# Key sums on TensorE, nine gradient steps ahead of the attention loop, and other queues for stores and transposes

## The chip, the cores and the metric

The kernel runs on one core of one Trainium2 chip. The core has five engines with instruction queues of their own: TensorE (PE in the profile; its weight loads are PEld), VectorE (DVE), ScalarE (ACT), GpSimd (POOL) and SyncE (SP), which here only issues DMAs. Sixteen DMA engines move the data. The metric is the device time of one execution in microseconds, as a median of several runs; less is better.

## The reference

The reference is one transformer block with linear attention and a gated feed-forward network (FFN), and its full backward pass. Tokens S = 2048, width D = 640, H = 32 heads of 20, FFN width F = 1728, all in bfloat16. The forward part, cut to what matters here:

```python
qkv = split_heads(layernorm(x) @ wqkv)              # q, k, v
phi = lambda t: jnp.where(t > 0, t + 1, jnp.exp(t)) + 1e-6
pq, pk = phi(q), phi(k)
kv  = jnp.einsum("bhsd,bhse->bhde", pk, v)
z   = jnp.einsum("bhsd->bhd", pk)                    # sum over all tokens
num = jnp.einsum("bhqd,bhde->bhqe", pq, kv)
den = jnp.einsum("bhqd,bhd->bhq", pq, z)[..., None] + 1e-6
h   = x + merge_heads(num / den) @ wo
xh  = layernorm(h)
h2  = h + (silu(xh @ w_gate) * (xh @ w_up)) @ w_down
```

`jax.vjp` then takes a given `grad_out` back to x and the five weight matrices. The seven outputs are h2 and these six gradients.

## The kernel before

The 2048 tokens are 16 tiles of 128. Matrices stay in SBUF as bfloat16 with 128 partitions; products are made in four PSUM tiles (`mm`, tag "mm"), which all stages share, each two banks wide. A PSUM tile is free again when ScalarE or VectorE has read it.

The stages in order of time are these.

1. Layer norm of x, q and k for each token tile, and phi (the loop that ends at line 379). `pk` holds phi(k), `pqa` holds phi(q). The function `phi(which, t, n)` works on n token tiles on VectorE, and after each fourth tile issues stores of the result from SyncE.
2. The sum z over all tokens, on VectorE (lines 465 to 472): FP32 additions over pairs of token tiles, a halving, and a split into a bfloat16 value `zs[0]` and a rest `zs[1]`. `z_bcast` multiplies both by a matrix of ones on TensorE, which puts z on all partitions (`zb`). Beside it TensorE makes Y = xn^T pk (`ps_y`, five row blocks), from it `KVT` (`ps_kvt`, lines 502 to 514, masked to heads by VectorE) and from that the combined matrix `W2` (`ps_w2t`, then a DMA transpose).
3. The normalisation of phi(q) by the denominator, four token tiles at a time: `norm_den` and `norm_mul`, on VectorE. `tr_pqs` then transposes the normalised tiles into `pqsT` with DMAs issued by SyncE.
4. The attention loop (lines 539 to 581). For each token tile t: ten matmuls `ps_a`; VectorE adds x (`xr`, loaded by SyncE) and so makes h in place, then layer-norm statistics; GpSimd makes the reciprocal deviation; two tiles later VectorE makes `hn` and SyncE transposes it into `hnT`. h itself goes to DRAM (`scr_h1`), issued by GpSimd. An `xr` buffer is free for the next load once `hn` is made and the store of h has landed; there are six buffers of that tag.
5. The FFN, in four column groups g of 448, 448, 448 and 384 columns (lines 603 to 704), starting with `pg`, then the backward pass.

Between the matmuls of stages 2 to 4 stand 24 *dm steps* (`dm_steps`, lines 393 to 407): each multiplies two token tiles of the transposed `grad_out` by a column group of `w_down`^T (`ps_dm`, 20 matmuls), and ScalarE copies the result out of PSUM. Groups 0 and 1 have 448 columns and stay in SBUF; the last eight steps have 384 columns and go to DRAM by a store that ScalarE issues (`scr_dm`, line 406). `dm(n)` puts n steps at a place in TensorE's order: twelve stand ahead of the attention loop, one between the halves of its first tile, and eleven in the loop, where t = 3, 7, 11 and 15 have none.

The order of the work on an engine is written out by hand in blocks (`manual_schedule`) for the engines that the block names: there the instructions run in the order of the program. On the other engines, and between two such blocks, a scheduler places them. `load_wgu(0)`, the first FFN weights, is written behind the loop; its two buffers are those of `wdT` and `wdT3`, the weights of the dm steps, so it needs step 16 to have run.

Of the kernel before, what the change touches and what calls it, by code (L numbers as in the profile page):

```python
# [8 lines left out]
FP32 = mybir.dt.float32  # L9
BF16 = mybir.dt.bfloat16  # L10
ALU = mybir.AluOpType
# [9 lines left out]
def kernel(  # L21
# [208 lines left out]
    with tc.manual_schedule(engines={EngineType.Pool}):  # L230
        ident = const.tile([P, P], BF16, name="ident")
        make_identity(nc, ident[:])
        nhalf = const.tile([P, 4], FP32, name="nhalf")
        nc.vector.memset(nhalf[:], -0.5)
        ones = const.tile([P, P], BF16, name="ones")
        nc.vector.memset(ones[:], 1.0)
        E = const.tile([P, D], BF16, name="E")
    zpad = const.tile([P, 4, 64], BF16, name="zpad")
    nc.vector.memset(zpad[:], 0.0)
    mask = const.tile([P, 160], BF16, name="mask")  # L240
# [67 lines left out]
    def phi(which, t, n=2):  # L308
        e = (pk, pqa)[which][:, t:t + n, :]
        nc.vector.tensor_scalar(out=e, in0=e, scalar1=1.0, scalar2=1e-6, op0=ALU.min, op1=ALU.add)  # L310
        last = nc.vector.tensor_tensor(out=e, in0=e, in1=rr[:, 2 * which + t // 2 % 2, t % 2:t % 2 + n, :], op=ALU.add)
# [7 lines left out]
        return last.ins  # L319

    PIECES = ((0, 3), (3, DT))

    with tc.manual_schedule(engines={EngineType.PE, EngineType.DVE, EngineType.Activation, EngineType.Pool}):
# [33 lines left out]
        for t in range(2, ST):  # L357
            if t == 2:
                ln1_stats(4)
            if t > 3 and t + 3 < ST:  # L360
                ln1_stats(t + 3)
            kq_mm(t, 0, (lambda: copy1(t + 1)) if t + 1 < ST else None)
            if t == 2:
                ln1_stats(5)
            if t == 3:
                ln1_stats(6)
            if t == ST - 1:
                phi(0, t - 1, 1)
            kq_mm(t, 1)
            if t == 3:  # L370
                phi(1, 0)
            elif t == ST - 1:
                last_phi = phi(0, t, 1)
            elif t > 3:
                phi(t % 2, t - 2 - t % 2)
            if t + 2 < ST:
                ln1_xn(t + 2)
            if ST - NC - 1 <= t < ST - 1:
                ln1_xn(t - ST + NC + 1)

    dm_t = {0: strips.tile([P, ST, GM], BF16, name="dm0", tag="S")}

# [26 lines left out]
    def dm(n):  # L411
        for _ in range(n):
            next(dms, None)

    def masks():
        nc.gpsimd.memset(mask[:], 1.0)
        for c0, n, p0 in ((0, 6, 0), (120, 2, 88)):
            m = mask[:, c0:c0 + n * Dh]
            for sign in (1, -1):
                nc.gpsimd.affine_select(  # L420
                    out=m, in_=m, pattern=[[-sign * Dh, n], [0, Dh]], compare_op=ALU.is_ge, fill=0.0,
                    base=-p0 if sign > 0 else p0 + Dh - 1, channel_multiplier=sign)
# [7 lines left out]
    def hb4(ap):  # L430
        return ap.rearrange("p t (h e) -> p t h e", e=Dh)

    def norm_den(t):

        pq = pqa[:, t:t + 4, :]
        tz = tzs[:, t % 8:t % 8 + 4, :]
        nc.vector.tensor_tensor(out=tz, in0=pq, in1=zb[:].unsqueeze(1).to_broadcast([P, 4, D]), op=ALU.mult)
        den = small.tile([P, 4, H], FP32, name="den", tag="den", bufs=2)
        nc.vector.tensor_reduce(out=den[:], in_=hb4(tz), axis=AX.X, op=ALU.add)
        nc.vector.tensor_scalar(out=den[:], in0=den[:], scalar1=1e-6, scalar2=None, op0=ALU.add)  # L440
        nc.vector.reciprocal(out=rall[:, t:t + 4, :], in_=den[:])

    def norm_mul(t):
        pq = pqa[:, t:t + 4, :]
        nc.vector.tensor_tensor(out=hb4(pq), in0=hb4(pq), in1=bc4(rall[:, t:t + 4, :]), op=ALU.mult)

    def tr_pqs(t, n=4):
        for tt in range(t, t + n):
            nc.sync.dma_start_transpose(out=pqsT[:, :, tt * P:(tt + 1) * P], in_=pqa[:, tt, :])

    xrs = {}
# [3 lines left out]
            xrs[t] = wk("xr")  # L455
            nc.sync.dma_start(out=xrs[t][:], in_=x_v[:, t, :])

    with tc.manual_schedule(engines={EngineType.PE, EngineType.DVE, EngineType.SP, EngineType.Pool}):
        yk = strips.tile([P, DT * D + HG * P], BF16, name="yk", tag="S")
        Yt = yk[:, :DT * D].rearrange("p (k n) -> p k n", k=DT)  # L460
        KVT = yk[:, DT * D:].rearrange("p (j c) -> p j c", j=HG)
        z2 = tzs[:, 4:8].rearrange("p t d -> p (t d)").bitcast(FP32)
        zf = z2[:, :D]
        tok2 = pk.rearrange("p (t two) d -> p t (two d)", two=2)
        with tc.issue_after(last_phi):
            nc.vector.tensor_tensor(out=z2, in0=tok2[:, 0], in1=tok2[:, 1], op=ALU.add)
        for t in range(2, ST // 2):
            nc.vector.tensor_tensor(out=z2, in0=z2, in1=tok2[:, t], op=ALU.add)
        nc.vector.tensor_tensor(out=zf, in0=zf, in1=z2[:, D:], op=ALU.add)
        zs = [wk("zs"), wk("zl")]  # L470
        nc.vector.tensor_copy(out=zs[0][:], in_=zf)
        nc.vector.tensor_tensor(out=zs[1][:], in0=zf, in1=zs[0][:], op=ALU.subtract)
        for t in (ST - 4, ST - 2):
            phi(1, t)
        nc.vector.memset(KVT, 0.0)
        masks()

        def z_bcast():
            ps = mm("ps_zb")
            mm_row(ps, lambda k: ones[:], lambda k, n0, n1: zs[k][:, n0:n1], 2)  # L480
            nc.scalar.copy(out=half(zb[:]), in_=row(ps))
# [38 lines left out]
        for i in range(DT):  # L520
# [15 lines left out]
        h1s = {}  # L536
        h1_todo = []
        hnT_todo = []
        for t in range(ST + 2):
            if t < ST:  # L540
                xr = xrs.pop(t)
# [11 lines left out]
                h1_todo.append((t, xr))  # L553
# [12 lines left out]
            u = t - 2  # L566
            if u < 0:
                continue
# [15 lines left out]
    fA.close()  # L584
    fpool = wB.enter_context(tc.tile_pool(name="fpool", bufs=6))

    with tc.manual_schedule(engines={EngineType.SP}):
        dh2 = big.tile([P, ST, D], BF16, name="dh2", tag="B")
# [477 lines left out]
```

## Time and profile before

| what | value |
|---|---|
| median of 3 runs | 822.23 us (821.71 to 822.48) |
| the profiled execution | 821.71 us, its span 820.0 us |
| TensorE busy (PE) | 812.0 us, 99% of the span |
| VectorE busy (DVE) | 453.0 us, 55% |
| ScalarE busy (ACT) | 288.1 us, 35% |
| GpSimd busy (POOL) | 200.4 us, 24% |
| mean granted TensorE clock | 0.998 |
| DMA, mean over the span | 193 GB/s |
| DMA in 55 to 85 us | busy share 0.37, 114 GB/s |
| DMA in 118 to 124 us | busy share 1.00, 291 GB/s |
| DMA in 150.2 to 183 us | busy share 1.07, 204 GB/s |

The span is the time from the first to the last instruction; what the execution takes beyond it is its start and end. The stages have their own limits, so the mean shares say little about one of them. In the views that follow, a line of the order of time gives the start in us, the length in us, the engine, the line of the kernel, the operation, the tile written and the tile read, the shape and the number of instructions; in square brackets stands how long the engine was idle before it and what ended that. A "q" behind an engine's name is its queue, which waits and issues DMAs.

### The profile page before, as it was taken

The numbers are of one execution on the slowest core, as the hardware profiler recorded it, in microseconds if no ns is written. First come the engines' busy times: TensorE is split into PE (matmuls) and PEld (weight loads), VectorE is DVE, ScalarE is ACT, GpSimd is POOL, SyncE is SP. The second block draws the span as 40 slices with busy tenths as digits, with TensorE's granted clock in tenths as the row PEclk, the third lists the DMA queues.
The fourth block names the chain that finished last, engine by engine and source line by source line (L and its number), as shares of the span: only waits on it lengthen the run. The fifth ranks groups of instructions, "written<-read, shape, count | busy, mean of one in ns | idle before, by whom it ended". The sixth has DMA issues, their size and how long they took to land.

```text
span 820.0 us, 13924 instructions
## 1 busy us (share of the span) xinstructions
PE 812.0 (99%) x5508; PEld 522.5 (64%) x5508; DVE 453.0 (55%) x857; ACT 288.1 (35%) x405; POOL 200.4 (24%) x366
## 2 busy tenths in 40 slices
PE   9999998999999999999999999999999999999998
PEld 7776565545555555555566677777777777777676
DVE  7879986891078008810670148787793266631212
ACT  6972531570085025500741122322322133322010
POOL 4410043412422311221124611221120111112330
PEclk9999999999999999999999999999999999999999
DMA  9992789999859976894398757987498999999952
GB/s 302 198 327 72 171 185 264 223 210 210 217 141 210 235 202 135 212 263 94 97 222 192 264 119 207 232 199 191 99 259 164 176 144 187 170 186 267 258 151 79
DMA packets 276785, 158.61 MB, mean 193 GB/s; under 512 B 235052, under 2 KB 262829, under 8 KB 276720
## 3 DMA queue, kind: packets, MB, share of 16 engines
q1 hardware_dynamic: 251696, 82.12, 53.8%
q0 software_dynamic: 18512, 67.07, 26.1%
q10 hardware_dynamic: 6512, 8.54, 3.3%
q8 instruction: 43, 0.70, 0.3%
q14 instruction: 22, 0.18, 0.1%
HBM read 47.68 MB, written 53.66 MB: 124 GB/s over the span
## 4 chain that ended last, share of the span: by engine, by line
PE 94%; DMA 4%; DVE 1%; issue 0%; ACT 0%; SPq 0%; POOL 0%; DVEq 0%; POOLq 0%
PE ps_dw L684 21%; PE ps_dhn L109 14%; PE ps_dxn L936 8%; PE ps_o L998 7%; PE pg L612 6%; PE ps_kq L300 5%; PE ps_dwqk L109 5%; PE pu L617 5%; PE ps_dm L390 5%; PE ps_dk L109 3%; PE ps_gt L743 3%; PE ps_dp L109 3%; PE ps_y L487 3%; PE ps_a L545 2%; PE pdm L390 2%; DMA stg<-dd 2%
## 5 line engine op out<-in xcount | busy, mean ns | idle before, releaser
L109 PE MATMUL ps_dhn<-wgT,cols 128*128 128x320 bf16 x864 | 119.5, 299 | 0.0
L684 PE MATMUL ps_dw<-dd,hn 128*128 128x448 bf16 (+1 forms) x640 | 118.8, 346 | 0.0
L109 PEld LDWEIGHTS <-cols 128*128 128x128 bf16 x864 | 84.5, 98 | 32.9
L684 PEld LDWEIGHTS <-hn 128*128 128x128 bf16 x640 | 62.6, 98 | 54.2
L686 DVE CAST dwev<-ps_dw 128x896 bf16<-128x896 f32 (+3 forms) x12 | 10.9, 907 | 128.3 <-PE ps_dw L684 110.2
L649 POOL DMA_DIRECT2D scr_dT<-stg x64 | 34.6, 541 | 167.4 <-DMA stg<-dd 166.9
L686 ACT CAST dwev<-ps_dw 128x896 bf16<-128x896 f32 (+1 forms) x20 | 17.6, 878 | 160.0 <-PE ps_dw L684 151.2
L147 DVE CUSTOM_DVE_ANT_0 lb_a<-lb_dy,hn 128x640 bf16<-128x640 bf16 x32 | 26.4, 826 | 76.1 <-ACT lb_dy L145 76.1
L617 PE MATMUL pu<-wgu,hnT 128*128 128x448 bf16 (+1 forms) x320 | 63.6, 346 | 0.0
L612 PE MATMUL pg<-wgu,hnT 128*128 128x448 bf16 (+1 forms) x320 | 63.6, 346 | 0.0
L998 PE MATMUL ps_o<-wd,mT 128*128 128x320 bf16 (+3 forms) x462 | 61.1, 295 | 0.0
L684 PE MATMUL ps_dw<-m_s,dh 128*128 128x448 bf16 (+1 forms) x320 | 60.5, 346 | 0.4 <-DMA dh<-in_grad_out_dram 0.4
L936 PEld LDWEIGHTS <-ring 128*128 128x128 bf16 x480 | 47.0, 98 | 18.2
L998 PEld LDWEIGHTS <-mT 128*128 128x128 bf16 (+1 forms) x462 | 41.8, 97 | 17.4 <-issue 2.6
L936 PE MATMUL ps_dxn<-wqkvT,ring 128*128 128x320 bf16 x320 | 51.3, 299 | 0.0
L390 PE MATMUL ps_dm<-wdT,dh2T 128*128 128x448 bf16 (+1 forms) x240 | 47.5, 348 | 3.2 <-DVE xr L549 3.2
L390 PEld LDWEIGHTS <-dh2T 128*128 128x128 bf16 x320 | 31.2, 98 | 28.8 <-issue 4.0
L684 PEld LDWEIGHTS <-dh 128*128 128x128 bf16 x320 | 31.2, 98 | 27.8 <-DMA dh<-in_grad_out_dram 0.9
L617 PEld LDWEIGHTS <-hnT 128*128 128x128 bf16 x320 | 31.3, 98 | 27.1
L612 PEld LDWEIGHTS <-hnT 128*128 128x128 bf16 x320 | 31.3, 98 | 27.0
L300 PE MATMUL ps_kq<-wqk,xnT 128*128 128x320 bf16 x320 | 46.4, 299 | 0.0
L145 ACT ACTIVATE lb_dy<-ps_dhn,rstd 128x640 bf16<-128x640 f32 x16 | 12.7, 793 | 86.7 <-PE ps_dhn L109 86.7
(168 smaller groups left out, 1294.5 us busy)
## 6 DMA issues: line engine op xcount, KB each, us to landing
scr_dT<-stg POOLq DMA_DIRECT2D x48, 224.0 KB, 3.2
cols<-scr_dT POOLq DMA_DIRECT2D x6, 1728.0 KB, 9.1
scr_m<-m_s POOLq DMA_DIRECT2D x12, 448.0 KB, 4.6
cols<-scr_dT ACTq DMA_DIRECT2D x2, 1728.0 KB, 10.4
out_dram<-dwev POOLq DMA_DIRECT2D x30, 112.0 KB, 3.2
scr_dT<-stg POOLq DMA_DIRECT2D x16, 192.0 KB, 2.7
scr_pk<-pk SPq DMA_DIRECT2D x4, 640.0 KB, 7.0
scr_xnT<-xnT SPq DMA_DIRECT2D x4, 640.0 KB, 7.2
```

What stands on the lines that cost most here:

```text
L109: nc.tensor.matmul(ps[:, ci, :320], lhsT=lhs(k), rhs=rhs(k, *NCH[ci]), start=(start and k == 0), stop=(stop and k == n - 1))
L147: nc.vector.tensor_tensor_reduce(out=a[:], in0=dy[:], in1=xhat, scale=1.0, scalar=0.0, op0=ALU.mult, op1=ALU.add, accum_out=sums[:, 1:2])
L300: nc.tensor.matmul(ps[:, ci, :320], lhsT=xnT[:, t, k, :], rhs=wqk[:, k, w0 + n0:w0 + n1], start=(k == 0), stop=(k == DT - 1))
L390: nc.tensor.matmul(ps[:, c, :w], lhsT=dh2T[:, kt, (t + c) * P:(t + c + 1) * P], rhs=wdT[:, kt, o:o + w], start=(kt == 0), stop=(kt == DT - 1))
L487: nc.tensor.matmul(ps[:, ci, :320], lhsT=xn[:, t, i * P:(i + 1) * P], rhs=pk[:, t, n0:n1], start=(t == 0), stop=(t == ST - 1))
L612: nc.tensor.matmul(pg[:, c, :w], lhsT=hnT[:, kt, (t + c) * P:(t + c + 1) * P], rhs=wg[:, kt, 0:w], start=(kt == 0), stop=(kt == DT - 1))
L617: nc.tensor.matmul(pu[:, c, :w], lhsT=hnT[:, kt, (t + c) * P:(t + c + 1) * P], rhs=wg[:, kt, w:2 * w], start=(kt == 0), stop=(kt == DT - 1))
L649: nc.gpsimd.dma_start(out=scr_dT[t + c, :, KO[g]:KO[g] + GK[g], :], in_=stg[:, :GK[g], :])
L684: nc.tensor.matmul(ps[:, c, :w], lhsT=lhs(t), rhs=rhs(t), start=(t == 0), stop=(t == ST - 1))
L686: last = copy(out=ev[:, :len(parts), :w], in_=ps[:, :len(parts), :w])
L936: nc.tensor.matmul(ps[:, ci, :320], lhsT=lhs[:, i, :], rhs=rhs[:, i, n0:n1], start=(k == 0 and i == 0), stop=(k == 2 and i == DT - 1))
L998: nc.tensor.matmul(po(t, ci), lhsT=mTs[t // 4][r, t % 4, j, :], rhs=wd[r, j, n0:n1], start=(t, ci) not in opened, stop=last)
```

## The change

The diff does the following.

- z is summed by TensorE: 32 matmuls with 32 columns of ones as weights, four quarters of the PSUM partitions in turn, between the halves of the first `ps_y` block. All 32 rows of a quarter hold the same sum, so the broadcast uses ones divided by 32 (`ones32`). ScalarE and VectorE make the split into `zs[0]` and `zs[1]` from PSUM. The FP32 additions on VectorE are gone.
- The last two `phi(1, ...)` run in the first stage's loop, ahead of the z work.
- The head masks are built on GpSimd, kept in the program's order, after the broadcast.
- `norm_den` and `norm_mul` become one function, `normalise`. Tiles 0 to 7 are normalised and transposed before the `xr` loads and `ps_kvt`, tiles 8 to 15 after `ps_w2t`; all transposes into `pqsT` are issued ahead of the loop.
- Nine dm steps stand ahead of the loop instead of twelve; in the loop there is one after each tile until the 24 are used up.
- The store of h (`scr_h1`) is issued by ScalarE at step t = u + 2, instead of by GpSimd a tile later than it is made.
- `hnT` is allocated ahead of the loop, and each tile of it is transposed in the step in which its `hn` is made. Before, the first four steps issued none, and later ones up to two.
- GpSimd's order in this part is no longer by hand. The pool `fpool` is opened, and `fA` closed, before the dm steps.

```diff
@@ (constants)
+    ones32 = const.tile([P, P], BF16, name="ones32")
+    nc.vector.memset(ones32[:], 1.0 / H)
@@ (first stage, in the loop over t)
             elif t == ST - 1:
-                last_phi = phi(0, t, 1)
+                phi(0, t, 1)
+                phi(1, t - 3)
+                phi(1, t - 1)
...
+    fA.close()
+    fpool = wB.enter_context(tc.tile_pool(name="fpool", bufs=6))
...
-    def norm_den(t):
+    def normalise(t):
...
-    def norm_mul(t):
-        pq = pqa[:, t:t + 4, :]
         nc.vector.tensor_tensor(out=hb4(pq), in0=hb4(pq), in1=bc4(rall[:, t:t + 4, :]), op=ALU.mult)
...
-    with tc.manual_schedule(engines={EngineType.PE, EngineType.DVE, EngineType.SP, EngineType.Pool}):
+    with tc.manual_schedule(engines={EngineType.PE, EngineType.DVE, EngineType.SP}):
...
-        with tc.issue_after(last_phi):
-            nc.vector.tensor_tensor(out=z2, in0=tok2[:, 0], in1=tok2[:, 1], op=ALU.add)
-        for t in range(2, ST // 2):
-            nc.vector.tensor_tensor(out=z2, in0=z2, in1=tok2[:, t], op=ALU.add)
-        nc.vector.tensor_tensor(out=zf, in0=zf, in1=z2[:, D:], op=ALU.add)
         zs = [wk("zs"), wk("zl")]
-        nc.vector.tensor_copy(out=zs[0][:], in_=zf)
-        nc.vector.tensor_tensor(out=zs[1][:], in0=zf, in1=zs[0][:], op=ALU.subtract)
-        for t in (ST - 4, ST - 2):
-            phi(1, t)
-        nc.vector.memset(KVT, 0.0)
-        masks()
...
+        def z_sum():
+            ps = mm("ps_z")
+            for ci, (n0, n1) in enumerate(NCH):
+                for t in range(ST):
+                    q = t % 4 * H
+                    nc.tensor.matmul(ps[q:q + H, ci, :320], lhsT=ones[:, :H], rhs=pk[:, t, n0:n1],
+                                     start=(t < 4), stop=(t >= ST - 4))
+            nc.scalar.copy(out=half(zs[0][:]), in_=row(ps))
+            nc.vector.tensor_tensor(out=half(zs[1][:]), in0=row(ps), in1=half(zs[0][:]), op=ALU.subtract)
+            nc.vector.memset(KVT, 0.0)
...
-                if (i, ci) == (2, 1):
-                    z_bcast()
+                if (i, ci) == (0, 0):
+                    z_sum()
             nc.scalar.copy(out=half(Yt[:, i, :]), in_=row(ps))
+            if i == 0:
+                ps_z = mm("ps_zb")
+                mm_row(ps_z, lambda k: ones32[:], lambda k, n0, n1: zs[k][:, n0:n1], 2)
+                nc.scalar.copy(out=half(zb[:]), in_=row(ps_z))
+                masks()
             if 0 < i < 4:
                 dm(1)
         dm(1)
-        norm_den(0)
-        norm_mul(0)
-        tr_pqs(0)
-        norm_den(4)
+        for t in (0, 4):
+            normalise(t)
+            tr_pqs(t)
         for t in range(6):
             load_xr(t)
...
-        norm_mul(4)
...
-        tr_pqs(4)
         for t in (8, 12):
-            norm_den(t)
-            norm_mul(t)
-            if t < 12:
-                tr_pqs(t)
-        dm(5)
+            normalise(t)
+            tr_pqs(t)
+        dm(2)
 
         hn = big.tile([P, ST, D], BF16, name="hn", tag="B")
+        hnT = big.tile([P, DT, S], BF16, name="hnT", tag="B")
...
-                if t > 0 and t % 4 != 3:
+                if t > 0:
                     dm(1)
-            while h1_todo and h1_todo[0][0] < t:
-                v, h1 = h1_todo.pop(0)
-                nc.gpsimd.dma_start(out=scr_h1_v[:, v, :], in_=h1[:])
             if t > 2:
                 load_xr(t + 3)
-            if t < 4:
-                tr_pqs(12 + t, 1)
-            if t == 3:
-                hnT = big.tile([P, DT, S], BF16, name="hnT", tag="B")
...
             h1, mv = h1s.pop(u)
+            nc.scalar.dma_start(out=scr_h1_v[:, u, :], in_=h1[:])
             nc.vector.tensor_scalar(out=hn[:, u, :], in0=h1[:], scalar1=mv[:, 0, 0:1],
                                     scalar2=rstd2[:, u:u + 1], op0=ALU.subtract, op1=ALU.mult)
-            hnT_todo.append(u)
-            for v in hnT_todo[:0 if t < 4 else 2]:
-                hnT_todo.pop(0)
-                nc.sync.dma_start_transpose(out=hnT[:, :, v * P:(v + 1) * P], in_=hn[:, v, :])
+            nc.sync.dma_start_transpose(out=hnT[:, :, u * P:(u + 1) * P], in_=hn[:, u, :])
```

More of the change, by code (lines that the diff above doesn't have):

```diff
@@ L310, in phi @@
         nc.vector.tensor_scalar(out=e, in0=e, scalar1=1.0, scalar2=1e-6, op0=ALU.min, op1=ALU.add)
-        last = nc.vector.tensor_tensor(out=e, in0=e, in1=rr[:, 2 * which + t // 2 % 2, t % 2:t % 2 + n, :], op=ALU.add)
+        nc.vector.tensor_tensor(out=e, in0=e, in1=rr[:, 2 * which + t // 2 % 2, t % 2:t % 2 + n, :], op=ALU.add)
         if (t + n) % 4 == 0:
@@ L318, in phi @@
                 nc.sync.dma_start(out=scr_xnT[sl].rearrange("t p k c -> p t k c"), in_=xnT[:, sl])
-        return last.ins
     PIECES = ((0, 3), (3, DT))
@@ L415, in masks @@
     def masks():
-        nc.gpsimd.memset(mask[:], 1.0)
+        tc.keep_in_program_order(nc.gpsimd.memset(mask[:], 1.0))
         for c0, n, p0 in ((0, 6, 0), (120, 2, 88)):
@@ L419, in masks @@
             for sign in (1, -1):
-                nc.gpsimd.affine_select(
+                tc.keep_in_program_order(nc.gpsimd.affine_select(
                     out=m, in_=m, pattern=[[-sign * Dh, n], [0, Dh]], compare_op=ALU.is_ge, fill=0.0,
-                    base=-p0 if sign > 0 else p0 + Dh - 1, channel_multiplier=sign)
+                    base=-p0 if sign > 0 else p0 + Dh - 1, channel_multiplier=sign))
     pqsT = big.tile([P, DT, S], BF16, name="pqsT", tag="B")
@@ L441, in norm_den, with tr_pqs @@
         nc.vector.reciprocal(out=rall[:, t:t + 4, :], in_=den[:])
-    def norm_mul(t):
-        pq = pqa[:, t:t + 4, :]
         nc.vector.tensor_tensor(out=hb4(pq), in0=hb4(pq), in1=bc4(rall[:, t:t + 4, :]), op=ALU.mult)
-    def tr_pqs(t, n=4):
-        for tt in range(t, t + n):
+    def tr_pqs(t):
+        for tt in range(t, t + 4):
             nc.sync.dma_start_transpose(out=pqsT[:, :, tt * P:(tt + 1) * P], in_=pqa[:, tt, :])
@@ L461 @@
         KVT = yk[:, DT * D:].rearrange("p (j c) -> p j c", j=HG)
-        z2 = tzs[:, 4:8].rearrange("p t d -> p (t d)").bitcast(FP32)
-        zf = z2[:, :D]
-        tok2 = pk.rearrange("p (t two) d -> p t (two d)", two=2)
-        with tc.issue_after(last_phi):
-            nc.vector.tensor_tensor(out=z2, in0=tok2[:, 0], in1=tok2[:, 1], op=ALU.add)
-        for t in range(2, ST // 2):
-            nc.vector.tensor_tensor(out=z2, in0=z2, in1=tok2[:, t], op=ALU.add)
-        nc.vector.tensor_tensor(out=zf, in0=zf, in1=z2[:, D:], op=ALU.add)
-        zs = [wk("zs"), wk("zl")]
-        nc.vector.tensor_copy(out=zs[0][:], in_=zf)
-        nc.vector.tensor_tensor(out=zs[1][:], in0=zf, in1=zs[0][:], op=ALU.subtract)
-        for t in (ST - 4, ST - 2):
-            phi(1, t)
-        nc.vector.memset(KVT, 0.0)
-        masks()
[L478 to L481, printed above, removed]
+        zs = [wk("zs"), wk("zl")]
+        def z_sum():
[8 more added lines that the diff above has]
+            nc.vector.memset(KVT, 0.0)
         for i in range(DT):
@@ L526 @@
             nc.sync.dma_start_transpose(out=W2[:, :, i * P:(i + 1) * P], in_=W2T[:, i, :])
-        tr_pqs(4)
         for t in (8, 12):
-            norm_den(t)
-            norm_mul(t)
-            if t < 12:
-                tr_pqs(t)
-        dm(5)
+            normalise(t)
+            tr_pqs(t)
+        dm(2)
         hn = big.tile([P, ST, D], BF16, name="hn", tag="B")
+        hnT = big.tile([P, DT, S], BF16, name="hnT", tag="B")
         h1s = {}
-        h1_todo = []
-        hnT_todo = []
         for t in range(ST + 2):
@@ L552 @@
                 ln_rstd(mv, rstd2, t, 1)
-                h1_todo.append((t, xr))
                 h1s[t] = (xr, mv)
-                if t > 0 and t % 4 != 3:
+                if t > 0:
                     dm(1)
-            while h1_todo and h1_todo[0][0] < t:
-                v, h1 = h1_todo.pop(0)
-                nc.gpsimd.dma_start(out=scr_h1_v[:, v, :], in_=h1[:])
             if t > 2:
                 load_xr(t + 3)
-            if t < 4:
-                tr_pqs(12 + t, 1)
-            if t == 3:
-                hnT = big.tile([P, DT, S], BF16, name="hnT", tag="B")
             u = t - 2
@@ L575 @@
             h1, mv = h1s.pop(u)
+            nc.scalar.dma_start(out=scr_h1_v[:, u, :], in_=h1[:])
             nc.vector.tensor_scalar(out=hn[:, u, :], in0=h1[:], scalar1=mv[:, 0, 0:1],
                                     scalar2=rstd2[:, u:u + 1], op0=ALU.subtract, op1=ALU.mult)
-            hnT_todo.append(u)
-            for v in hnT_todo[:0 if t < 4 else 2]:
-                hnT_todo.pop(0)
-                nc.sync.dma_start_transpose(out=hnT[:, :, v * P:(v + 1) * P], in_=hn[:, v, :])
-    fA.close()
-    fpool = wB.enter_context(tc.tile_pool(name="fpool", bufs=6))
+            nc.sync.dma_start_transpose(out=hnT[:, :, u * P:(u + 1) * P], in_=hn[:, u, :])
     with tc.manual_schedule(engines={EngineType.SP}):
```

## The prediction

> **What bounds the kernel now.** I read the waits of TensorE first, then the chain of waits, then stretches of the attention loop, then its instructions in order of time. The waits of TensorE, with total, number and longest in us, are these:
>
> ```profile
> PE ps_dm L390 <- DVE xr L549: 3.2, 1, 3.2
> PE ps_warm L329 <- POOL ident masks.py:199: 1.6, 1, 1.6
> PE ps_dw L684 <- DMA dh<-in_grad_out_dram: 0.4, 1, 0.4
> ```
>
> TensorE is busy for 99% of the span, so every matmul added is paid for in full, and what another engine saves counts only where TensorE waits. The second of these waits is the start of the kernel and the third the first weight gradient; inside the changed part it waits once, for 3.2 us. The chain (start, length) gives the places around it and the price of one kind of matmul that the change adds:
>
> ```profile
> 93.49 9.46 PE ps_dm L390 x50
> 150.26 1.91 PE pg L612 x10
> 618.82 1.20 PE ps_dz L876 x32
> ```
>
> The attention loop begins at 93.49 + 9.46 = 102.95 and the FFN at 150.26, so it takes 47.31. Its matmuls need less. The chain shows a half tile `ps_a` of ten matmuls as 1.36, a `ps_dm` step as 1.89 at 448 columns and about 1.63 at 384. Sixteen tiles (21.76), four steps of 1.89 and eight of 1.63 make 42.36. So 4.95 us are lost. Where they go is seen in the loop (stretch, length, busy us of each engine, granted clock, DMA share, GB/s):
>
> ```profile
> 133.00:136.00 3.00, 3.00 (x23) 2.09 (x22) 0.21 (x1) 0.00 (x0) 1.46 (x3) 1.00 1.11 196
> 136.00:140.00 4.00, 0.83 (x7) 0.43 (x5) 1.37 (x3) 0.80 (x1) 0.00 (x0) 1.00 1.16 285
> 140.00:145.00 5.00, 5.00 (x24) 2.77 (x23) 4.83 (x13) 0.80 (x1) 2.92 (x6) 0.66 0.99 289
> ```
>
> From 133 VectorE and ScalarE nearly stop, the DMA engines are full, TensorE stops at 136.3, and then it works at a granted clock of 0.66. The gap is 3.17, so the slow clock is the other 1.8. The Trainium skill ("TensorE: Matmul & The Clock Gate", Part 1) says that an idle window of about 3.4 us halves the clock until TensorE has been busy again; the trace agrees with the halving, after a gap of 3.17, and by that rule a gap well under a window would cost its own length alone. In order of time:
>
> ```profile
> 127.07 0.61 SPq L185 DMA_DIRECT2D wgu<-in_B_w_gate_dram  x1
> 127.73 0.74 SPq L186 DMA_DIRECT2D wgu<-in_B_w_up_dram  x1
> 130.63 0.86 SPq L456 DMA_DIRECT2D xr<-in_A_x_dram  x1
> 131.27 0.80 ACT L404 CAST dmst<-ps_dm 128x768 bf16<-128x768 f32 x1 [2.82 <-DMA xr<-in_A_x_dram]
> 133.42 2.88 PE L545 MATMUL ps_a<-wvo,pqsT 128*128 128x320 bf16 x20
> 137.72 0.37 ACTq L406 DMA_DIRECT2D scr_dm<-dmst  x1
> 138.59 0.82 DVE L549 TENSOR_TENSOR xr<-ps_a,xr 128x640 bf16<-128x640 f32 x1 [5.38 <-DMA xr<-in_A_x_dram]
> 139.47 2.73 PE L390 MATMUL ps_dm<-wdT,dh2T 128*128 128x384 bf16 x10 [3.17 <-DVE xr L549]
> ```
>
> SyncE issues the first FFN weights at 127.07 and 127.73 (1.1 MB), and the `xr` load for tile 10 behind them at 130.63. The chain has that load as 7.84 long, so it lands at 138.47. VectorE could have added tile 10 about 133.2 and adds it at 138.59; TensorE has meanwhile filled all four PSUM tiles (two attention tiles stand side by side at 133.42, since the step at t = 11 is left out) and takes up step 139.47 when the add ends.
>
> **The change, part by part.** *z on TensorE.* Seven FP32 adds, a half add, a cast and a subtraction leave VectorE: 1.48 + 9.12 + 0.83 + 0.49 + 0.82 = 12.7 us, from 55.74 to 68.63, all beside matmuls, so nothing is saved directly. TensorE gains 32 matmuls of 32 weight columns. The same shape, `ps_dz`, takes 1.20 for 32; as 32 full-width ones (`ps_y`, 4.35 for 32) it would be 4.35. The new ones write the four quarters in turn as `ps_dz` does, so I take **+1.20**, and keep +4.35 as the other end. The Trainium skill ("TensorEngine Tiling", Key Properties) says that a change of tiling mode drains TensorE; a quarter of 4.35 is 1.09, so in this trace such drains have at most 0.11 for `ps_dz`, already inside the row.
>
> The broadcast of z (four matmuls, 0.54, in both) now waits for ScalarE's cast and VectorE's subtraction. z ends at 54.9 + 2.2 + 1.2 = 58.3; 0.69 and 0.82 after it make 60.0; the second half of `ps_y` covers TensorE until 60.4. In front on VectorE stand two `phi(1, ...)` of 1.31 each, moved here, done at 58.5. So 0, with 0.4 to spare; without that cover up to 1.7. Mask building goes later on GpSimd, which idles from 47 to 108; its 128x128 constant memset (0.17) lies in VectorE's wait for x at the start. Both 0.
>
> *Normalisation and transposes.* A block of four tokens tiles takes 8.4 us of VectorE (89.41 to 97.77). Now z arrives at 62, so blocks 0 and 4 end at 79, ahead of the `ps_kvt` masks at 87.9 (86.7 + 1.2), and `pqsT` 4 to 7 is transposed on SyncE by about 84, before the `xr` loads rather than behind the W2 transposes. Those loads issue near 84.2, against 85.23 now; the five transposes of W2 issue until 97.8 now and land 2.7 after their start, so the last lands near 99.3, or 100.5 with the 1.2; the half tile that reads it is wanted at 98.5 + 0.68 + 1.89 = 101.1. 0, with 0.6 to spare. Blocks 8 and 12 end at 87.9 + 16.8 = 104.7.
>
> *Nine steps ahead, not twelve.* Three steps of 1.89 move into the loop: no matmul is added or lost, but the loop starts at 102.95 + 1.20 - 5.68 = 98.5 while VectorE is at the blocks until 104.7. Tiles 0 and 1 wait in PSUM. By turn, tile 2 takes tile 0's place; TensorE wants it at 98.5 + 0.68 + 1.89 + 2.04 + 1.89 = 105.0, VectorE has added tile 0 at 105.6. **+0.6**; 0 if another place is free, and 1.5 if VectorE is a microsecond later. Next late would be tile 3, at 109.6, against its place free near 108: nothing.
>
> *The wait at 136.* In the new order every attention tile is followed by a step, until t = 14. Tile t's place is wanted again after three more tiles (1.63 + 1.36 + 1.63 = 4.6); an add takes 0.82, so `xr` may be 3.8 late before TensorE waits. SyncE enters the loop with all `pqsT` transposes issued: they end near 110, landed near 113, and `hnT` starts there against 118.41 now, while the loop is 4.4 earlier; it lags one microsecond less, and `hnT` no longer goes two at a time ahead of an `xr` load. The FFN weights need the place of `wdT`, free when step 16 has run: t = 6, near 122. `xr` 10 landed 11.4 after the weights' issue now (138.47 - 127.07), so near 133.4 to 134; tile 10 ends at 132.3. It is 1 to 2 late, under 3.8. So the **4.95** go, and I leave **+0.5** for transfers that are slower than this; the ends are 0 and the whole 4.95, and the value nearer to the first is taken because the slack is twice the lateness.
>
> *`scr_h1` from GpSimd to ScalarE.* Sixteen issues of about 0.37 (the `scr_dm` row at 137.72) join ScalarE, whose steps take 0.8 to 0.9 of 3: 0 as work. GpSimd loses 16 of 0.63. What a wait at such an issue costs is a rival below.
>
> Sum, on the profiled execution's 821.71 (span 820.0, 1.7 around it): +1.20 + 0.6 - 4.95 + 0.5 = -2.65, so 819.1. That run was the fastest of three, 0.5 under the median 822.23; with the same step the median comes to **819.6**.
>
> **The rivals.** *The wait stays* (0.17). For: the DMA share is 1.0 or more from 118 on whatever the order, and the same 1.1 MB goes ahead of the same loads. Against: the slack of 3.8, where two adjoining tiles left about none. Then 822.23 + 1.20 + 0.6 = **824.0**, or 823.4 without the 0.6.
>
> *ScalarE is held by its stores* (0.22), the slower side. ScalarE empties every `ps_dm`; a store queued there holds the cast behind it. Now it carries 8 stores in the loop; the one at 137.72 belongs to a cast that ended at 132.07 and waited 5.65, and the waits of ScalarE name `hnT` (6.1 us) as what let it go, a SyncE transfer. With 24 stores such waits are met three times as often. A `ps_dm` place is wanted after 4.35, the cast takes 0.8: it decides from a hold of 3.5 on. A hold as long as the slowest `hnT` landing, 9.1, costs 5.6 and then the slow clock's 1.8: 822.23 - 4.95 + 1.20 + 0.6 + 7.4 = **826.5**. Against: ScalarE's DMA at 121.16 waited for nothing but its cast, and SyncE lags less.
>
> *The FFN weights go out behind the last `hnT`* (0.05): issued near 151, landing after 8 to 9, TensorE waits ten and more: **830**. For: SyncE is a queue in order. Against: it issued them in the middle of the loop now. *z doesn't overlap its quarters* (0.06): 819.6 + 3.15 = **822.8**.
>
> **How the numbers follow.** My forecast has 0.50, with its own range 818.0 to 821.4 (no 0.6 and no 0.5; or 1.5 and 1.5). A measurement of this kernel tells about 0.2% from no change: faster is under 820.6, slower over 823.9. The forecast gives 0.41 faster and 0.09 same; the first rival 0.07 same and 0.10 slower; the others 0.06 same and 0.27 slower. Together 0.41, 0.22, 0.37. The range runs from 817.6 to 827.0, leaving out the late weights and half of the longest holds.
>
> **What would show it.** Right: `ps_z` x32 near 57 lasting 1.2; `ps_zb` without a wait; the loop's first `ps_a` near 98.5; no TensorE wait over 1 us before the FFN, which starts near 147; granted clock 1.00 throughout. Wrong: a wait of `ps_dm` or `ps_a` for `xr` as long as now (first rival); long ScalarE gaps in front of its DMA issues, with TensorE waiting for ScalarE (second); `pg` waiting for `wgu` (third); `ps_z` near 4.

## The result and the profile after

| | before | after |
|---|---|---|
| median, 6 runs each | 822.36 us (821.62 to 822.93) | 818.06 us (817.39 to 818.60) |
| ratio | | 0.9948 (95%: 0.9935 to 0.9960) |
| profiled execution, its span | 821.71, 820.0 | 817.39, 815.5 |
| mean granted TensorE clock | 0.998 | 1.000 |

The kernel is faster by 0.52%, which is more than the 0.2% that a measurement of it can tell. The waits of TensorE in the changed kernel (total, number, longest in us) are one line long:

```profile
PE ps_warm L330 <- POOL ident masks.py:199: 1.4, 1, 1.4
```

The start of the kernel is all that is left. The 3.2 for `xr` are gone, and so are the 0.4 of the first weight gradient. The chain of waits (start, length) gives the price of z and the ends of the stages:

```profile
54.73 2.17 PE ps_y L482 x16
56.91 1.20 PE ps_z L472 x32
58.11 2.28 PE ps_y L482 x16
60.39 0.54 PE ps_zb L109 x4
...
98.26 0.68 PE ps_a L539 x5
...
104.76 1.36 PE ps_a L539 x10
...
146.24 1.89 PE pg L593 x10
```

The row of the 32 matmuls of z is 1.20 long, and `ps_zb` follows the second half of `ps_y` with no gap. That half takes 2.28, where the half ahead of z takes 2.17: another 0.11 that z brings with it. The loop takes 146.24 - 98.26 = 47.98. Its matmuls need 16 x 1.36 + 7 x 1.89 + 8 x 1.63 = 48.03: nothing is lost in it, where before 47.31 were spent on 42.36 of work. The same three stretches of the loop as before (stretch, length, busy us of each engine, granted clock, DMA share, GB/s) show what replaced the gap:

```profile
133.00:136.00 3.00, 3.00 (x22) 1.98 (x21) 2.25 (x6) 0.87 (x2) 0.87 (x2) 1.00 1.16 343
136.00:140.00 4.00, 4.00 (x30) 2.67 (x28) 2.84 (x8) 1.60 (x2) 1.39 (x4) 1.00 1.16 310
140.00:145.00 5.00, 5.00 (x35) 3.21 (x34) 3.91 (x8) 0.89 (x2) 1.23 (x3) 1.00 0.91 255
```

The DMA engines are as full as they were (share 1.16, 310 to 343 GB/s), yet TensorE is busy throughout at a granted clock of 1.00. So the change did not take traffic away. What it changed is seen in the order of time:

```profile
112.52 1.21 SPq L565 DMA_TRANSPOSE hnT<-hn  x1
...
122.47 0.38 SPq L185 DMA_DIRECT2D wgu<-in_B_w_gate_dram  x1
...
124.20 0.95 SPq L459 DMA_DIRECT2D xr<-in_A_x_dram  x1
125.20 0.48 SPq L186 DMA_DIRECT2D wgu<-in_B_w_up_dram  x1
...
131.36 0.82 DVE L543 TENSOR_TENSOR xr<-ps_a,xr 128x640 bf16<-128x640 f32 x1 [0.68 <-PE ps_a L539]
```

SyncE reaches the first `hnT` at 112.52, where it was at 118.41 before, and issues the `xr` of tile 10 at 124.20 instead of 130.63. The matmuls of tile 10 end at 131.2 in this kernel and at 131.8 in the one before. So the load was issued 7.0 ahead of the end of its tile, where it had been 1.2 ahead, and VectorE adds the tile 0.2 after its last matmul (131.36) instead of 6.8 after it (138.59). From issue to landing the load takes 5.8 here and 7.8 in the kernel before, so the earlier issue is the larger part of what it gained. One thing in these lines was not in the forecast: the two weight transfers no longer stand together, and the `xr` of tile 10 goes out between them. The scheduler places them; why it drew them apart no run shows.

### The profile page after: what moved, and what is told of

Its sections match the earlier page's. It is cut to its first block, busy times and chain, and to the rows that moved or that the text cites. A ratio compares the mean times of both kernels' runs of the same rounds, so it can differ in the third digit from the quotient of the medians.

```text
span 815.5 us, 13979 instructions
## 1 busy us (share of the span) xinstructions
PE 811.0 (99%) x5540; PEld 522.2 (64%) x5540; DVE 442.7 (54%) x849; ACT 288.9 (35%) x406; POOL 193.4 (24%) x350
## 4 chain that ended last, share of the span: by engine, by line
PE 99%; POOL 0%; ACT 0%; issue 0%; DVE 0%; POOLq 0%
PE ps_dw L665 21%; PE ps_dhn L109 14%; PE ps_dxn L917 8%; PE ps_o L979 7%; PE pu L598 7%; PE pg L593 7%; PE ps_kq L302 5%; PE ps_dwqk L109 5%; PE ps_dm L396 5%; PE ps_y L482 3%; PE ps_gt L724 3%; PE ps_dp L109 3%; PE ps_dk L109 3%; PE ps_a L539 3%; PE pdm L396 2%; PE ps_warm L330 1%
```

## The experiments

All times are medians, with the ratio to the kernel before as it was run beside them. "Late" is the start of VectorE's add minus the end of the tile's matmuls (read as the start of the matmul that follows at once; 0.2 is the least), "ahead" is how long before that end the `xr` load is issued.

**x1. The weights loaded three tiles later.**

```diff
+            if t == 9:
+                wgu[0] = load_wgu(0)
...
-        wgu = {0: load_wgu(0)}
```

> The kernel before, with the first FFN weights issued three tiles later in the attention loop (behind xr 12 instead of xr 9); nothing else. Theory (the wait at 136 us is xr 10 queued behind 1.1 MB of weights): TensorE's wait of 3.2 us and the slow clock behind it go, the span falls from 820.0 by 4 to 5, to about 815.5. Rival (the DMA engines are full and some xr is late in any order, or ScalarE's stores hold it): a wait of 3 us or more stays somewhere in the loop, span 819 to 821.

Median 817.93 (816.91 to 821.63), ratio 0.9968 (0.9953 to 0.9983). The profiled execution took 820.95, and its waits of TensorE name the same pair:

```profile
PE ps_a L546 <- DVE xr L550: 3.0, 1, 3.0
```

Its chain shows that the wait moved along with the weights, which went out at 135.2 and 135.9, to the next `xr` behind them, that of tile 13:

```profile
138.26 7.66 DMA xr<-in_A_x_dram
...
146.92 2.73 PE ps_a L546 x10
```

The load takes 7.66 here against 7.84 before: what makes it late is what stands ahead of it. That the wait would vanish was wrong, and a wait of 3 is what the rival forecast too. What speaks for the theory is the place: tiles 6 to 12 are 2.0 late at most, and the first that is later (tile 13, 6.9) is the one behind the weights. The median is 3.0 under this one execution, and five of ten executions took 816.9 to 817.5, so others may have had a shorter wait or none.

**x2. The spacing of the steps alone.** Nine steps ahead of the loop, one after every tile; z and the transposes as before.

```diff
-        dm(5)
+        dm(2)
...
-                if t > 0 and t % 4 != 3:
+                if t > 0:
```

> The kernel before, with nine steps ahead of the loop and one after every tile; z, stores and SyncE's order stay as they were. Theory that spacing gives the slack: the wait for xr falls to under 1.5 us, with up to 3.4 at the loop's start since VectorE is busy with the normalisation until 106; span 816 to 820. Rival that SyncE's order of transposes and loads is what made xr late: the wait for xr stays at 2 us or more with the slow clock behind it, and the loop's start adds to it; span 820 or more.

Median 817.36 (817.0 to 819.6), ratio 0.9959 (0.9942 to 0.9976), span 815.6. The waits of TensorE beside the start:

```profile
PE ps_a L545 <- DMA wvo<-wvo: 0.5, 1, 0.5
PE ps_dm L390 <- ACT dmst L404: 0.2, 1, 0.2
```

No wait for `xr`, though the loads of tiles 8 to 12 are only 1.9 to 2.4 ahead and up to 3.7 late. This edit is not quite alone, however: with other steps around it the scheduler also drew the two weight transfers apart (126.89 and 129.45, an `xr` load between them). It leaves open which of the two did it; x3, x9 and x12 bear on that. The 0.5 is W2, whose transposes land later than the earlier loop wants it. At the loop's start VectorE is still at the normalisation, so tiles 0 to 2 are 4.2 to 5.6 late, and TensorE doesn't wait for them.

**x3. The changed kernel without the spacing.** The edit of x2 backwards, in the kernel after.

> The changed kernel, with twelve steps ahead and none at t = 3, 7, 11, 15, as before. If the spacing removed the wait, it comes back: 3 us and the slow clock, span 819 to 820. If SyncE's order did (transposes into pqsT all issued ahead, hnT one at a time), nothing comes back: span 815.2 to 816.0.

Median 817.87 (817.57 to 818.11), ratio 0.9956 (0.9939 to 0.9972), span 816.0, no wait but the start. The loads of tiles 8 to 13 are 3.1 to 4.9 ahead and at most 2.1 late. So the rest of the change removes the wait as well. Its chain also prices a hold of ScalarE:

```profile
126.79 5.71 DMA scr_h<-xr
132.50 0.79 ACT dmst L410
133.34 1.79 PE ps_dm L396 x10
```

ScalarE was idle for 7.1 ahead of this cast, by its list of waits until a store of h had landed. The step that it copies had ended at 128.71, so the cast was held for 3.8. TensorE took up its next step as the cast ended, at 133.34 where tile 10 had ended at 133.06: a loss of 0.3, too short for its list of waits.

**x4. The stores of h back on GpSimd**, at the place where the changed kernel has them.

```diff
-            nc.scalar.dma_start(out=scr_h1_v[:, u, :], in_=h1[:])
+            nc.gpsimd.dma_start(out=scr_h1_v[:, u, :], in_=h1[:])
```

> The changed kernel, with the store of h issued by GpSimd at the same place instead of by ScalarE. Theory (ScalarE's stores cost nothing on the path): span 815.5 within 0.5; if GpSimd's stores were what made the last dh2 load late, the 0.4 us wait of the first weight gradient for it is back. Rival (the move to ScalarE frees xr buffers sooner and so took the wait away): a wait of ps_dm or ps_a for xr of 2 us or more, span 818 or more.

Median 817.18 (817.09 to 817.23), ratio 0.9948 (0.9933 to 0.9963), span 815.5. The ratio is that of the changed kernel: no price of moving the stores can be told here, in either direction. The 0.4 of the first weight gradient is not back either.

**x5. Only SyncE's order**, on the kernel before: all transposes into `pqsT` ahead of the loop, one `hnT` per tile.

```diff
-            if t < 12:
-                tr_pqs(t)
+            tr_pqs(t)
...
-            for v in hnT_todo[:0 if t < 4 else 2]:
+            for v in hnT_todo[:1]:
```

> The kernel before, with SyncE's order alone changed as in the change: all transposes into pqsT ahead of the loop, hnT allocated there and transposed one tile at a time. z stays on VectorE, twelve steps ahead, h stored by GpSimd. If SyncE's order alone removes the wait: no TensorE wait over 1 us in the loop, span 814.5 to 816 (the z on VectorE saves 1.2 against the changed kernel). If what removed it with the spacing undone was VectorE's earlier normalisation: the wait is back, 2 to 3 us and the slow clock, span 818 to 820.

Median 819.18 (818.42 to 821.56), ratio 0.9970 (0.9958 to 0.9982), span 817.4. The waits of TensorE beside the start:

```profile
PE ps_dm L390 <- DVE xr L549: 1.3, 1, 1.3
PE ps_a L545 <- DVE xr L549: 1.1, 2, 0.6
```

Part of the wait stays. With z still on VectorE the normalised tiles come late, so the transposes that now stand ahead of the `xr` loads hold them: the load of tile 6 goes out at 119.07 against 113.79 in the changed kernel, and those of tiles 8 to 10 are only 0.6 to 1.6 ahead. The weights are drawn apart in this kernel too (126.01 and 128.72), so that alone is not enough.

**x6. SyncE's order and the spacing, z on VectorE.** x5 with a step after every tile and ten ahead of the loop.

> The kernel before, with SyncE's order and with ten steps ahead and one after every tile; z stays on VectorE. Theory that the 1.20 of z on TensorE is the only loss of the change and the rest of it only takes waits away: span 815.5 - 1.2 = 814.3, or up to 815 with a short wait at the loop's start, where VectorE is busy until 106. Rival that the late normalisation (z on VectorE) gives the 1.2 back: a wait of 1 us or more at the loop's start, span 815.3 or more.

Median 819.09 (815.96 to 820.96), ratio 0.9962 (0.9946 to 0.9978), span 817.3.

```profile
PE ps_a L545 <- DVE xr L549: 2.3, 2, 1.6
PE ps_dm L390 <- ACT dmst L404: 0.4, 1, 0.4
```

Two parts that each take time off do not add up: the loads of tiles 8 to 10 are only 0.3 to 1.3 ahead, and the tiles up to 5.7 late. Against the changed kernel it lacks the early z with the earlier normalisation, and it has a tenth step ahead of the loop; which of these takes the lead away was not tried apart. The place of the stores of h, the other difference, cost nothing in x4.

**x7 and x8. SyncE's lead taken away in steps.** The changed kernel with `xr` loaded two tiles ahead, and one tile ahead, instead of three (one execution each).

```diff
-        for t in range(6):
+        for t in range(5):
...
-                load_xr(t + 3)
+                load_xr(t + 2)
```

> The changed kernel, with each xr load issued two tiles ahead of its use instead of three (3.0 us later). Theory that an xr may be 3.8 us late before TensorE waits: VectorE waits for xr 9 or 10 by up to 3 us, TensorE not or under 0.5; span 815.3 to 816.2. Rival that there is no such slack: TensorE waits 1.5 us or more, span 817 or more.

817.11, span 815.2, no wait of TensorE beside the start. VectorE's adds in order of time, of tiles 9 and 10, now do wait:

```profile
129.84 0.82 DVE L543 TENSOR_TENSOR xr<-ps_a,xr 128x640 bf16<-128x640 f32 x1 [2.12 <-DMA xr<-in_A_x_dram]
133.68 0.82 DVE L543 TENSOR_TENSOR xr<-ps_a,xr 128x640 bf16<-128x640 f32 x1 [1.54 <-issue]
```

They are 1.95 and 2.8 late, and that is free: PSUM holds the tiles meanwhile.

> The changed kernel, with each xr load issued one tile ahead of its use (6 us later than in the changed kernel). Theory: behind the weights xr comes 5 to 6 us late, past the slack of 3.8, so TensorE waits 1 to 3 us there, with part of the slow clock; span 817 to 820. Rival that the load behind the weights doesn't set it: span under 816.5.

826.69, span 824.8. Now the loads are issued 0.8 to 3.1 after the end of their tiles:

```profile
PE ps_a L539 <- DVE xr L543: 3.7, 5, 1.5
PE ps_dw L665 <- DVE m_s L626: 1.7, 2, 1.6
PE pu L598 <- DVE xr L543: 1.5, 1, 1.5
PE pg L593 <- ACT m_s L619: 0.9, 1, 0.9
```

The direction was right and the size too small: the span is 9.3 over that of the changed kernel. The waits shown add up to 7.8, of which only 3.7 are the loop's own `ps_a`; the rest falls on the FFN (`pu`, `pg`, `ps_dw`), where the wait of `pu` names the same late `xr`. What makes the other 1.5 these lines don't show.

**x9. The weights in ten pieces**, two after each `xr` load of t = 6 to 10, on the kernel before.

```diff
+            if 6 <= t < 6 + DT:
+                k = t - 6
+                nc.sync.dma_start(out=wgu[0][:, k, 0:GM], in_=B_w_gate[k * P:(k + 1) * P, 0:GM])
+                nc.sync.dma_start(out=wgu[0][:, k, GM:2 * GM], in_=B_w_up[k * P:(k + 1) * P, 0:GM])
```

> The kernel before with one edit: the first FFN weights (1.1 MB) go in ten pieces of 115 KB, two after each xr load of t = 6 to 10, in place of two transfers issued together. Theory (a load that is needed now is queued behind a long one that isn't): each xr load has at most 0.23 MB of weights ahead of it, so each is 1 to 3 us late, under the 3.8 from which TensorE waits: no wait of ps_dm or ps_a for xr over 1 us, span 815 to 816.5, median 817 to 818. Rival (the DMA engines are full from 118 on, the same bytes make the loads late whatever the pieces): lateness builds up over tiles 9 to 13 and TensorE waits 2 us or more in all, span 818 to 820.

Median 817.83 (816.33 to 819.32), ratio 0.9955 (0.9939 to 0.9971), span 815.4. The only wait of TensorE in the loop and, from the chain, the load of tile 10:

```profile
PE ps_a L546 <- ACT dmst L404: 0.4, 1, 0.4
```

```profile
129.22 4.39 DMA xr<-in_A_x_dram
```

Spacing, z and SyncE's order are as before, the bytes are the same and the load is issued 2.2 ahead, not much earlier than the 1.2 of before. But it takes 4.39 in place of 7.84, and no tile is more than 3.7 late. ScalarE was held as well when TensorE stopped in the kernel before, and it still is here (first the kernel before, then x9):

```profile
138.13 0.80 ACT L404 CAST dmst<-ps_dm 128x768 bf16<-128x768 f32 x1 [6.06 <-DMA hnT<-hn]
137.12 0.80 ACT L404 CAST dmst<-ps_dm 128x768 bf16<-128x768 f32 x1 [6.05 <-DMA wgu<-in_B_w_gate_dram]
```

ScalarE stands still as long as it did, and only 0.4 is left of 3.2, so ScalarE did not make the rest. This edit takes away the cause of the old wait: 1.1 MB in two transfers directly ahead of a load that is wanted.

**x10. The spacing and the pieces together**, x2 with the edit of x9.

> The kernel before with a step after every tile (nine ahead) and the same ten pieces; z stays on VectorE. Theory: neither the wait for xr nor the long holds of ScalarE (4.4 and 3.6 with the spacing alone), so the loop takes its 42.4 plus the three steps and nothing else: span 814.4 to 815.3, median 816 to 817, under both kernels by 1 us or more. Rival (pieces only spread the same lateness): waits of 0.7 or more as with the spacing alone, span 815.6 to 817.

Median 818.21 (817.55 to 820.0), ratio 0.9969 (0.9954 to 0.9984), span 818.1: not better than either edit by itself. From tile 4 on the adds are 2.2 late at most, but TensorE waits for another engine:

```profile
PE ps_dm L390 <- ACT dmst L404: 1.7, 1, 1.7
```

ScalarE's instructions in order of time show why (in brackets: idle before, and what ended it):

```profile
134.46 0.38 ACTq L406 DMA_DIRECT2D scr_dm<-dmst  x1
134.89 0.80 ACT L404 CAST dmst<-ps_dm 128x768 bf16<-128x768 f32 x1 [5.04 <-DMA wgu<-in_B_w_gate_dram]
```

The cast stood behind a store that ScalarE issued only at 134.46, though the cast that made its data had ended at 129.84; by the profile it was a piece of the weights, a transfer of SyncE's, that let it go. This is the second rival of the prediction, in another kernel and at a smaller price.

**x11. z on TensorE alone**, in the kernel before.

> The kernel before with one edit: z summed by TensorE (32 matmuls in four quarters), cast and subtraction behind it; the steps, SyncE's order and the stores stay. Theory (z costs 1.20 and the wait goes by the spacing or by SyncE's order together with the early z, not by an early VectorE alone): the wait for xr at tile 10 stays at 2 to 3.5 us and the slow clock behind it, span 820.3 to 821.5. Rival (an early VectorE is all that is needed): wait under 0.5, span 816 to 817. If z cost 4.35 the first rises by 3.

Median 820.94 (819.70 without the longest execution), ratio 0.9998 (0.9969 to 1.0028), and the executions lie far apart (817.57 to 827.15 without the longest). In the profiled one (819.70, span 818.0):

```profile
PE ps_dm L392 <- DVE xr L553: 2.2, 1, 2.2
```

The weights stand together ahead of the load of tile 10 again, which is 1.2 ahead and 5.8 late. An early VectorE is not enough, and here 1.20 us more of matmuls meet the old wait. In the stretches around this gap the granted clock stayed at 1.00:

```profile
138.00:139.00 1.00, 0.00 (x0) 0.00 (x0) 0.52 (x1) 0.57 (x1) 0.00 (x0) 1.00 1.16 369
139.00:140.00 1.00, 0.64 (x4) 0.39 (x4) 0.97 (x3) 0.00 (x0) 0.00 (x0) 1.00 1.14 306
140.00:141.00 1.00, 1.00 (x9) 0.60 (x7) 0.97 (x4) 0.00 (x0) 0.35 (x2) 1.00 1.16 315
```

**x12. The spacing, with the stores of the steps on GpSimd**, and ten steps ahead of the loop.

```diff
-                    nc.scalar.dma_start(out=scr_dm_v[:, t:t + 2, :], in_=dst[:, :, :w])
+                    nc.gpsimd.dma_start(out=scr_dm_v[:, t:t + 2, :], in_=dst[:, :, :w])
```

> The kernel before with a step after every tile (ten ahead of the loop), the eight scr_dm stores issued by GpSimd in place of ScalarE, and z left on VectorE. Theory: the waits that were left with the spacing alone were ScalarE's holds at those stores (0.2; 1.7 with the weights in pieces) and the W2 transposes (0.5, which the tenth step covers); without them the loop takes only its matmuls, span 814.4 to 815.2, median 816.2 to 817.3, under the changed kernel by about the 1.20 of z, and the runs lie closer together. Rival (ScalarE's holds follow from the same full DMA engines, and whoever issues the stores holds what is queued behind them, on GpSimd the rstd of the next tile): TensorE waits 0.5 to 2 us for VectorE, span 815.5 to 817, median 817.3 to 819.

Median 819.52 (817.93 to 822.62), ratio 0.9976 (0.9961 to 0.9991), span 817.9: by its median slower than x2, though the two intervals overlap. The wait that stays is one that neither side named.

```profile
PE ps_a L545 <- DVE xr L549: 2.8, 2, 1.8
```

ScalarE is no longer held and GpSimd is not either; the wait is the one for `xr`. SyncE in order of time shows it:

```profile
126.52 0.52 SPq L456 DMA_DIRECT2D xr<-in_A_x_dram  x1
127.08 0.50 SPq L186 DMA_DIRECT2D wgu<-in_B_w_up_dram  x1
127.68 3.23 SPq L581 DMA_TRANSPOSE hnT<-hn  x1
131.00 0.53 SPq L456 DMA_DIRECT2D xr<-in_A_x_dram  x1
```

The weights go 2.6 earlier than in x2 (gate at 124.30). The longer wait, 1.8, is for tile 9. Its load stands behind the first half of the weights, goes out 2.3 ahead, and takes 7.9 to land, where the load in that place took 4.0 in x2; why, the runs do not show. Then a transpose that takes 3.23 to issue stands ahead of the load of tile 10, which is 0.8 ahead, and the tile 6.9 late.

No version that was run is clearly ahead of the changed kernel. The medians of x1, x2, x3, x4, x9 and x10 and the one execution of x7 lie within a microsecond of it.

## Why the prediction was right, and where its sizes were off

The forecast was 819.6, by a sum of -2.65; 818.06 was measured, and the profiled span fell by 4.5. The direction is as forecast, and so is the main mechanism: the wait at 136 and the slow clock behind it are gone, for the price of z. Two terms of the sum came to 0, one was a little too small, and small gains were missing from it.

- **z on TensorE, +1.20**: 1.20 for its row and 0.11 more in the half of `ps_y` behind it, 1.31 in all (in x11 the three halves behind z take 6.63, where 3 x 2.17 would be 6.51). I took the 0.11 inside the row of `ps_dz` for the whole price of such a switch. Behind `ps_dz`, too, the 30 matmuls of `ps_dkvt` take 1.54, where the 30 of `ps_kvt` take 1.43. The other end, 4.35, is out: the four quarters overlap. The broadcast's 0.4 to spare held: the subtraction was done by 59.70 and `ps_zb` started at 60.39.
- **The place in PSUM at the start of the loop, +0.6**: 0. This step failed. I let tile 2 take the place of tile 0 "by turn". VectorE's add of tile 0 ended at 105.21, yet tile 2 started at 104.76: a place that a step had left free was given to it. ScalarE had copied the step that began at 98.94 out of PSUM by 101.78, and the other three places were still held.
- **The wait at 136, -4.95 with 0.5 left over**: the 4.95 went in full, so the 0.5 is 0. The lateness was forecast at 1 to 2 and was 0.2, the least there is; `xr` 10 landed not 11.4 after the weights' first issue, as in the chain before, but 7.5 after it (124.20 + 5.8 - 122.47), as it went out between the two transfers. So the changed kernel never draws on the slack of 3.8 that the forecast leaned on; SyncE's lead, which it named second, was enough.
- **Not in the sum**: the 0.4 of the first weight gradient, which is gone, and the first `ps_y`, at 54.73 instead of 55.05. The wait at the start is 1.6 in the other kernels made from the one before and 1.4 in all those made from the changed one, so 0.2 may be the mask building, which left GpSimd's start; that was not tried by itself. The first `ps_y` starts anywhere from 54.53 to 55.29 in the former and from 54.45 to 55.01 in the latter, so 0.3 is no more than the spread. The 0.4 was not tried either; it came and went in the other kernels (0.7 in x10, none in x2).

With these the sum is 1.31 - 4.95 - 0.4 - 0.3 = -4.34, against -4.5; the rest isn't placed.

The forecast's own range has a slip. Without the 0.6 and the 0.5 its terms give 822.23 + 1.20 - 4.95 = 818.5, and the text has 818.0. The 818.06 lies under what the terms reach, by about the 0.4 and 0.3 that were not in the sum; that the range as written holds it is luck.

The cause of the loss, weights ahead of `xr`, is shown by x9 (cut up, the wait goes) and fits x1 (moved, the wait moves with them). The point from which lateness costs, 3.8, was worked out for a step after every tile, and from tile 6 on it holds: at the first wait for `xr` of each kernel, the lateness of the tile waited for less the wait is 3.6 to 4.2.

| | tile | late | wait | difference | steps |
|---|---|---|---|---|---|
| before | 10 | 6.8 | 3.2 | 3.6 | as before |
| x1 | 13 | 6.9 | 3.0 | 3.9 | as before |
| x5 | 8 | 4.4 | 0.5 | 3.9 | as before |
| x11 | 10 | 5.8 | 2.2 | 3.6 | as before |
| x6 | 8 | 5.5 | 1.6 | 3.9 | after every tile |
| x8 | 6 | 4.4 | 0.2 | 4.2 | after every tile |
| x12 | 9 | 5.7 | 1.8 | 3.9 | after every tile |

From tile 6 on no tile is over 3.7 late in the six kernels without a wait for `xr` (after, x2, x3, x4, x7, x9). But the table also shows a step of the prediction that was wrong: against the first rival it says that two adjoining tiles had left about no slack. They left 3.6 (before, x11), so the new spacing gave next to none; what changed is the lateness. At the loop's start the point lies higher: tile 1 is 5.6 late in x2 at no cost, and 6.0 late in x10, where TensorE waits 0.2 for it at 108.94.

What the change as a whole did is then not one of its parts. The spacing, with the weights drawn apart, is enough (x2), though x12, with a tenth step and another queue for the stores, waits again; all but the spacing is enough (x3); SyncE's order alone, or z alone, is not (x5, x11), and SyncE's order with the spacing is not while z is late (x6). The weights are apart in x5, x6 and x12 too, and these wait 2.3 to 2.8 for `xr`. What they lack is lead: 0.4 to 2.3 at the tiles waited for. With the whole change the loads of tiles 8 to 15 are 6.3 to 8.0 ahead, and x7 gives about half of that away at no cost. So the 1.31 for z buys no time that can be told from x2, which goes without it (the intervals of the two ratios overlap). What may be bought is margin: six executions of the changed kernel lie within 1.2 us and four of x4 within 0.2, while x1, x5, x6 and x12, which have the wait, spread over 3.1 to 5.0. That is not shown, though: x2 and x9, whose profiled executions have no such wait, spread over 2.6 and 3.0.

Of the rivals, *the wait stays* fell with the first list of waits. *ScalarE is held by its stores* was real as a mechanism, and its point, "from a hold of 3.5 on", was right. From the end of a step to its cast, holds of 3.8 (x3), 3.9 (x2), 4.1 (x9) and 5.4 (x10) cost TensorE about 0.3, 0.2, 0.4 and 1.7. In the changed kernel the longest hold in the last eight steps was 2.5 and cost nothing. *The weights behind the last `hnT`* fell with their issue at 122.47 and 125.20, *z doesn't overlap* with the 1.20.

## What to carry to other kernels

Read a late load by what stands ahead of it on its issuing queue, and compare its issue with the end of the work that needs it, not with the traffic on the DMA engines: these were as full after as before. Where a large transfer that nobody wants yet stands ahead of a small one that is wanted, cutting it into pieces between the small ones did as much here as reordering everything around it. And parts of a change that each remove the same wait are not to be added up: try each alone, and look where the scheduler put what was not ordered by hand.

## What the runs showed of the hardware

The clock. After gaps of 3.17 (before) and 3.0 (x1) TensorE worked at half the clock; after 2.2 (x11, above), 1.8 (x12), 1.7 (x10) and 1.6 (x6) its mean granted clock stayed at 1.00. In x1, the stretches after its gap:

```profile
147.00:148.00 1.00, 1.00 (x5) 0.59 (x5) 0.97 (x4) 0.80 (x1) 0.00 (x0) 0.53 1.10 370
148.00:149.00 1.00, 1.00 (x6) 0.53 (x4) 1.00 (x3) 0.00 (x0) 0.79 (x2) 0.50 1.20 328
```

Five or six matmuls per microsecond instead of eight to ten. So the wait of 3.17 cost 4.95 in the kernel before, and the one of 2.2 in x11 only itself. The Trainium skill ("TensorE: Matmul & The Clock Gate", Part 1) puts the idle window at about 3.4 us; by these runs 3.0 can be enough.

The price of a place in the queue. The same 164 KB load took 7.84 (before) and 7.66 (x1) behind 1.1 MB, and 4.39 behind pieces of 115 KB (x9), each time with the DMA engines full (share 1.12, 1.09 and 1.16 over those stretches). Behind the first half of the weights alone it took 4.0 (x2), 5.8 (after) and 7.9 (x12), so the bytes ahead are not all that counts. And by the profile a DMA that ScalarE issues stood still until a transfer issued by SyncE had landed (x10, ScalarE idle for 5.04), though the two share no data; which resource they share the traces do not show.
